# Attention and a Fourier layer on one core: the sums of the first Fourier stage are made earlier and kept in DRAM

## The chip, the cores and the metric

The kernel runs on one core of a Trainium2 chip. The time is device time in microseconds (us). The engines are TensorE (PE; PEld is its weight load), VectorE (DVE), ScalarE (ACT), GpSimd (POOL), and SyncE (SP), which issues every DMA of this kernel.

## The reference

Two independent halves share the inputs' shape of 2048 tokens by 1024, and their outputs are joined side by side:

```
qkv = x @ wqkv                         # 32 heads of 32
p = softmax(q k^T / sqrt(32)); o = p v
A = o @ wo
a, b = xB @ Wd_re^T, xB @ Wd_im^T      # Fourier matrices, hidden
B = C_re @ a - C_im @ b                # Fourier matrices, sequence
out = concat(A, B)
```

## The kernel before, in words

All products outside the attention ("fills") are in single precision. Each operand is split into a high and a low part (`halves`, L543), and each pair of operands costs three 128x128x512 matmuls: high by high, low by high, high by low. Products of 2x2 blocks are done with 7 instead of 8 block products, so that operands are often sums or differences of blocks.

The fills stand in one list that fixes their order: the projections q, k, v (`qkv`, L643, steps x = 0 to 11), the first Fourier stage (`dense1`, L1250: the input's transpose times the sequence matrices), the second (`dense2`), and the output projection. The attention's matmuls come in three streams: S (L1586, the pass that finds the maxima), T (L1711, the transposed scores) and V (L1741, probabilities by values). S, T and V are laid between the fills.

That order is made by a planner (`Plan`), which runs all engines on a clock of its own with a cost for each instruction. On POOL, DVE, ACT and SP it takes the ready operation with the lowest rank, which is the number of fill groups listed so far. Each engine then runs its list strictly in that order, SP too: a DMA that must wait holds all later DMAs. Tiles are numbered as the planner hands them out, whichever engine writes them, so the numbers of two engines tell which came first in its plan.

Steps that matter here:

- `fetch` (L488) makes a sum of blocks: a DMA for the first block (L511, into `raw`, or `er` while x < 5), one for each further block (L520, into `g`, or `raw` while x < 5), an add on POOL or DVE (L530), and, if the sum is used again, a DMA that stores it (L538). `raw` has 6 buffers, `g` 4, `er` 8; all are handed out in turn.
- `piece` (L559) fetches a stationary operand of 128x512 (four 128x128 weights) and splits it: the high half `h` on ACT (L549) or DVE (L550), the low half `l` on POOL or DVE (L553). `moving` (L585) does the same for the other operand, into `slot` tiles.
- `qkv` step x = 3: six groups on q and k, then eight on v (t = 0 to 7), each of 12 matmuls. Step x = 4 begins with three weights (two groups each), made from a block of `wqk` and a stored block `sq_d`.
- `dense1` runs its seven block products in the order 1, 2, 5, 6, 7, 4, 3. Products 1 and 3 are cut once more into seven (`split`, L1320), the others are whole (`simple`, L1269). The stationary sums of products 5, 6, 7 (and 3) were fetched at their own product: 8 pieces each in `simple`, 2 each in `split`. Sum 5 was stored in `s1_d`, 6 in `s2_d`, the base of product 3 in `s4_d` (made in product 7), the inner sums 5 and 6 in `w5_d`, `w6_d`.

Of the kernel before, what the change touches and what calls it, by code (L numbers as in the profile page):

```python
# [8 lines left out]
F32 = mybir.dt.float32  # L9
# [7 lines left out]
P = 128  # L17
# [207 lines left out]
def kernel(  # L225
# [168 lines left out]
    SPLIT = (1,3)  # L394
# [222 lines left out]
    class Acc:  # L617
# [5 lines left out]
        def at(self):  # L623
            return self.get()[:, self.half]
# [15 lines left out]
    CR = Ring(NCR)  # L640
    CR.users = [att_gate for _ in range(NCR)]

    def qkv():  # L643
        VR, SG = Ring(NV), Ring(2)
        sq, tx, t1x = ([[] for _ in range(8)] for _ in range(3))
# [267 lines left out]
        for x, (p, blocks, v) in enumerate(STEPS[:10]):  # L913
            spare[0] = x < 5
            if x == 0:
                where[0] = ahead
                W = []
                for c in range(4):
                    W.append(blocks_piece(c))
                    load_x(0, c)  # L920
                qk_groups(W, 0)
                for k in range(4, 8):
                    load_x(0, k)
                qk_groups(W, 1)
                for c in range(4):
                    load_v_weight(0, c)
            for i, b in enumerate(blocks if x else ()):
                where[0] = ahead if x < 5 else within
                W = piece(w_terms(p, lambda i, j: wqk[b + 8 * i][:, 4 * j : 4 * j + 4, :], sq_d[b], sq[b]), (sq_d[b], sq[b]) if p == 6 else None)
                if x > 5 and i == 0:  # L930
                    for k in range(4, 8):
                        load_x(x, k)
                qk_group(x, W, b, 0)
                qk_group(x, W, b, 1)
                if x < 5:
                    for k in range(8 * i // len(blocks), 8 * (i + 1) // len(blocks)):
# [12 lines left out]
            if x == 4:  # L949
                for u in ahead[0].users + slots[32:]:  # L950
                    att_gate.extend(u)
                for i in range(12, 16):
                    slots[i] = list(att_gate)
            if x == 9:
                for c in range(4):
                    load_v_weight(10, c)
        for x in (10, 11):
            for t in range(8):
                v_group(x, t)
                if x == 11 and t < 4:  # L960
                    load_x(11, 4 + t)
                elif x == 10 and t < 2:
                    for k in range(2):
                        load_x(10, 4 + 2 * t + k)
                elif x == 10 and 2 <= t < 6:
                    load_x(11, t - 2)
                    load_v_weight(11, t - 2)
        for b in range(8):
            W = [piece(w_terms(p, lambda i, j: wqk[b + 8 * i][:, 4 * j : 4 * j + 4, :], None, None)) for p in (7, 4)]
            for n in range(2):  # L970
                qk_group(10, W[0], b, n)
                qk_group(11, W[1], b, n)

    ORDER = (1, 2, 6, 7, 5, 3, 4)

# [272 lines left out]
    steps = [0]  # L1248

    def dense1():  # L1250
        s4 = [[[] for _ in range(2)] for _ in range(4)]
        t2 = [[[] for _ in range(8)] for _ in range(4)]
        s2 = [[[] for _ in range(2)] for _ in range(4)]
        s2_d = [[dram.tile([P, 4, P], F32, name=f"s2_d{m}_{k}") for k in range(2)] for m in range(4)]
        s4_d = [[dram.tile([P, 4, P], F32, name=f"s4_d{m}_{k}") for k in range(2)] for m in range(4)]
# [3 lines left out]
        s1, t1 = [[[] for _ in range(2)] for _ in range(4)], [[[] for _ in range(8)] for _ in range(4)]  # L1259
        s1_d = [[dram.tile([P, 4, P], F32, name=f"s1_d{m}_{k}") for k in range(2)] for m in range(4)]  # L1260
        t1_d = [[dram.tile([P, NB], F32, name=f"t1_d{n}_{c}") for c in range(8)] for n in range(4)]
        xq = lambda d, s: (xb[d, :, s : s + 4, :], [])
        cq = lambda e, s, n: (ct[e, s, :, n * NB : n * NB + NB], [])
        step = steps

# [2 lines left out]

        def simple(p):  # L1269
            def a(m, k):  # L1270
                q = lambda r, kk: xq(4 * r + m, 8 * kk + 4 * k)
                return split_a(p, q, (s1_d[m][k], s1[m][k]), (s2_d[m][k], s2[m][k]))

            def b(n, c):
                q = lambda k, e: cq(e, 8 * k + c, n)
                return split_b(p, q, (t1_d[n][c], t1[n][c]), (t2_d[n][c], t2[n][c]))

            keep_a = {5: lambda m, k: (s1_d[m][k], s1[m][k]), 6: lambda m, k: (s2_d[m][k], s2[m][k])}.get(p, lambda m, k: None)
            keep_b = {5: lambda n, c: (t1_d[n][c], t1[n][c]), 6: lambda n, c: (t2_d[n][c], t2[n][c])}.get(p, lambda n, c: None)
            A = {}  # L1280
            for n in range(4):
                z = step[0]
                step[0] += 1
                M = []

                def load(m, k):
                    if n == 0:
                        A[m, k] = held(fetch([P, 4, P], a(m, k), keep_a(m, k)), None if m < 2 else 12 + 2 * m + k)

                for k in range(2):  # L1290
                    load(0, k)
                    for c in range(4 * k, 4 * k + 4):
                        M.append(moving((8 * z + c) % 12, b(n, c), keep_b(n, c)))
                for m in range(1, 4):
                    for k in range(2):
                        load(m, k)
                for m in range(4):
                    h = DONE_IN.get(p)
                    out_to = to(h, m, n) if h else (None, None)
                    group(((chunk(A[m, k], c), (M[4 * k + c], whole)) for k in range(2) for c in range(4)), 8,  # L1300
                          outer(p, X[m][n], Y[m][n], *out_to, h is not None and h[1] == 1))
                    if p == 7 and 3 in SPLIT and m % 2:
                        i, k = divmod(2 * n + m // 2, 2)
                        fetch([P, 4, P], [(1, *xq(i, 8 + 4 * k)), (-1, s2_d[i][k], s2[i][k])], (s4_d[i][k], s4[i][k]))

        def stays():
            box = {}
# [10 lines left out]
            return k  # L1318

        def split(i):  # L1320
            def base_a(m, k):
                return (s4_d[m][k], s4[m][k]) if i == 3 else xq(m, 8 * (i - 1) + 4 * k)

            def base_b(c, n):
                return cq(*{1: (0, c), 2: (0, 8 + c), 3: (1, 8 + c)}[i], n)

            w, w_d = {}, {}
            for p in (5, 6):
                for n in range(2):
                    w[p, n], w_d[p, n] = [], dram.tile([P, 4, P], F32, name=f"w{p}_d{i}_{n}")  # L1330
# [5 lines left out]
            for j in WITHIN:  # L1336
# [481 lines left out]
    while nf < len(fills) or any(place[n] < len(s) for n, s in streams.items()):  # L1818
# [27 lines left out]
        held = False  # L1846
# [96 lines left out]
```

## Time and profile before

| | |
|---|---|
| median of 3 runs | 2926.0 us (2925.46 to 2927.98) |
| the profiled execution | 2924.82 us, its span 2923.0 us |
| PE, share of the span | 100% (weight loads 73%) |
| ACT, DVE, POOL | 79%, 77%, 38% |
| DMA, 16 engines | 67.8%; 636.24 MB |
| TensorE clock | 1.0 of full speed throughout |

Busy time of PE is read with care: a matmul of 512 columns is shown 389 ns long, though the next one starts 227 ns after it. So a gap in the rows of PE is shorter than the time that was really lost there.

### The profile page before, as it was taken

To read this page: it belongs to the slowest core of one execution; us is meant where nothing else is said; L and a number is where in the kernel's file an instruction comes from. 1 tells how busy PE (TensorE), PEld (TensorE's weight loads), DVE (VectorE), ACT (ScalarE), POOL (GpSimd) and SP (SyncE) were. 2 spreads that over 40 slices of the span, in tenths; PEclk is the share of its full clock that TensorE was granted. 3 is DMA by queue.
4 is the path that set the end of the run, shared out by engine and by line. 5 is a ranking of instruction groups with operands and counts; after the bars stand their busy time and mean duration, and the time that the engine had idled before them with its cause. 6 is when DMAs were issued, how large, how long until landed. Compare 5 with 4: busy or idle time off the path is not lost.

```text
span 2923.0 us, 46116 instructions
## 1 busy us (share of the span) xinstructions
PE 2911.5 (100%) x14826; PEld 2130.8 (73%) x14826; DVE 2260.2 (77%) x3072; ACT 2297.2 (79%) x4369; POOL 1107.2 (38%) x866
## 2 busy tenths in 40 slices
PE   9999999999999999999999999999999999999999
PEld 7887777776667776777776777777677777777787
DVE  7778888788889768777778787778877877876496
ACT  5348888888899888888888888988888888887532
POOL 2323335222365124243434342347613653342042
PEclk9999999999999999999999999999999999999999
DMA  9975658766687448678869775568735776663463
GB/s 340 372 241 186 201 183 280 231 214 223 220 263 227 146 136 274 219 241 273 277 224 286 227 240 170 155 192 281 231 98 172 255 238 189 188 189 123 124 241 140
DMA packets 444956, 636.24 MB, mean 218 GB/s; under 512 B 115726, under 2 KB 150286, under 8 KB 444590
## 3 DMA queue, kind: packets, MB, share of 16 engines
q1 hardware_dynamic: 444716, 633.29, 67.8%
q8 instruction: 120, 1.97, 0.3%
q14 instruction: 120, 0.98, 0.1%
HBM read 448.56 MB, written 184.57 MB: 217 GB/s over the span
## 4 chain that ended last, share of the span: by engine, by line
PE 94%; ACT 2%; DMA 2%; DVE 1%; issue 1%; SPq 0%; DVEq 0%; ACTq 0%
PE pd L433 43%; PE psT L1711 16%; PE psS L1586 15%; PE pd L1741 14%; PE psT L433 6%; ACT psS L1595 1%; ACT pt L1718 1%; DMA qs<-m_d 0%; DMA m_d<-lt 0%; DVE negm L1592 0%; DMA raw<-in_ct 0%; PE psT L455 0%; DMA er<-in_xa 0%; DMA qs<-qk_d 0%; DMA er<-in_wv 0%
## 5 line engine op out<-in xcount | busy, mean ns | idle before, releaser
L1592 DVE TENSOR_REDUCE negm<-psS 128x1 f32<-128x1024 f32 x1024 | 1242.4, 1220 | 255.9 <-PE psS L1586 244.6
L1595 ACT ACTIVATE psS<-psS,negm 128x1024 f32<-128x1024 f32 x1024 | 1230.0, 1201 | 75.2 <-DVE negm L1592 69.5
L1718 ACT ACTIVATE pt<-psT 128x512 f32<-128x512 f32 x1656 | 1000.8, 705 | 267.4 <-PE psT L1711 243.8
L433 PE MATMUL pd<-slot,h 128*128 128x512 f32 x2704 | 921.3, 390 | 0.0
L1711 PE MATMUL psT<-qs,ks 128*128 128x512 f32 x2048 | 794.5, 394 | 2.3 <-ACT pt L1718 1.3
L553 POOL TENSOR_TENSOR slot<-raw,slot 128x512 fp32r<-128x512 f32 x278 | 357.6, 1292 | 776.1 <-DVE slot L550 424.2
L433 PEld LDWEIGHTS pd<-slot,h 128*128 128x128 f32 x2704 | 507.5, 188 | 106.1 <-issue 0.8
L530 POOL TENSOR_TENSOR raw<-raw,g 128x512 f32<-128x512 f32 x321 | 414.8, 1302 | 428.4 <-issue 78.1
L433 PE MATMUL pd<-slot,l 128*128 128x512 f32 x1352 | 526.7, 390 | 0.0
L1711 PEld LDWEIGHTS psT<-qs,ks 128*128 128x128 f32 x2048 | 381.9, 188 | 142.0 <-issue 42.7
L1586 PE MATMUL psS<-ks,qs 128*128 128x512 f32 x1552 | 474.0, 391 | 2.5 <-ACT psS L1595 2.2
L433 PE MATMUL pd<-slot,slot 128*128 128x512 f32 x1560 | 436.3, 389 | 0.0
L1741 PE MATMUL pd<-pt,vt 128*32 128x512 f32 x3312 | 408.2, 594 | 0.0
L1586 PEld LDWEIGHTS psS<-ks,qs 128*128 128x128 f32 x1552 | 290.0, 188 | 67.0 <-ACT psS L1595 6.2
L433 PEld LDWEIGHTS pd<-slot,slot 128*128 128x128 f32 x1560 | 292.8, 188 | 60.8
L1595 ACT ACTIVATION_READ_ACCUMULATOR psS<-psS,negm 128x1 f32 x1024 | 328.2, 321 | 0.0
L433 PEld LDWEIGHTS pd<-slot,l 128*128 128x128 f32 x1352 | 253.8, 188 | 52.3
L1718 ACT ACTIVATE ptm<-psT 128x512 f32<-128x512 f32 x392 | 242.4, 716 | 48.9 <-PE psT L1711 47.1
L1741 PEld LDWEIGHTS pd<-pt,vt 128*32 128x32 f32 x3312 | 108.6, 110 | 231.8 <-issue 217.2
L553 POOL TENSOR_TENSOR l<-raw,h 128x512 fp32r<-128x512 f32 x105 | 135.5, 1290 | 224.5 <-PE psT L1711 79.0
L550 DVE CAST slot<-raw 128x512 fp32r<-128x512 f32 x364 | 168.0, 482 | 6.2 <-DMA raw<-in_wo 3.1
L1586 PE MATMUL psS<-ks,qx 128*128 128x512 f32 x496 | 150.1, 393 | 1.0 <-ACT psS L1595 1.0
(158 smaller groups left out, 2066.0 us busy)
## 6 DMA issues: line engine op xcount, KB each, us to landing
raw<-in_ct SPq DMA_DIRECT2D x212, 256.0 KB
g<-in_ct SPq DMA_DIRECT2D x148, 256.0 KB
raw<-ut_d SPq DMA_DIRECT2D x112, 256.0 KB
qk_d<-e SPq DMA_DIRECT2D x52, 512.0 KB
qs<-qk_d SPq DMA_DIRECT2D x128, 192.0 KB
ks<-qk_d SPq DMA_DIRECT2D x128, 192.0 KB
c<-xx_d SPq DMA_DIRECT2D x80, 256.0 KB
c<-u_d SPq DMA_DIRECT2D x72, 256.0 KB
```

The lines of the kernel that those rows point to most:

```text
L433: nc.tensor.matmul(box["ps"], a[1]((a[0].hi, a[0].lo)[u]()), b[1]((b[0].hi, b[0].lo)[v]()), start=k == 0, stop=k == n - 1)
L530: return (nc.gpsimd if e == "POOL" else nc.vector).tensor_tensor(out=dest(), in0=x, in1=y, op=ALU.add if sign > 0 and not turned else ALU. ...
L550: return nc.vector.tensor_copy(hi(), raw())
L553: return (nc.gpsimd if e == "POOL" else nc.vector).tensor_tensor(out=lo(), in0=raw(), in1=f(hi()), op=ALU.subtract)
L1586: nc.tensor.matmul(p[:, i * NB : i * NB + NB], (QX[0] if own else QS[h % 2])[:, qt * P : qt * P + P], KS[h % 2][:, c * 1024 + i * NB : c * ...
L1592: nc.vector.tensor_reduce(out=ST["negm"][:, c, qt : qt + 1], in_=box["p"], axis=AX.X, op=ALU.max, negate=True)
L1595: nc.scalar.activation(box["p"], box["p"], AF.Exp, bias=ST["negm"][:, c, qt : qt + 1], accum_out=ST["sums"][:, c, qt : qt + 1])
L1711: nc.tensor.matmul(box["p"], KS[h % 2][:, t * P : t * P + P], QS[h % 2][:, j * NB : j * NB + NB], start=True, stop=True)
L1718: nc.scalar.activation(box["t"], box["p"], AF.Exp)
L1741: nc.tensor.matmul(po["p"][j * DH : j * DH + DH, :], VT[h][:, k, :], box["t"], start=(k == t0), stop=(k == t), tile_position=(0, j * DH),)
```

## The change

`presum(key)` makes one stationary sum with `fetch` and always stores it, in a DRAM tile of its own (`sums_...` for the eight pieces of a whole product, `sum1_...` and `sum3_...` for the two of an inner one). `beside(what, n)` makes the next n sums of a list, and is called after groups of other stages: the eight inner sums of product 1 in the v groups of step x = 3; the eight sums 5 in the v groups of steps 10 and 11; the eight sums 6 in the q and k groups behind them; sums 7 and 3 (16) in product 2; the eight inner sums of product 3 in product 4. At their own product, `a` and `inner_a` then give one term, the stored sum, so that `fetch` is one DMA (L511) with no add.

The diff, cut to its core (the calls of `beside` stand inside the loops named above):

```diff
+    BESIDE = {"x":of_inner(1),"v":of_all(5),"qk":of_all(6),2:of_all(7)+of_all(3),4:of_inner(3)}
+    def presum(key):
+        what, i, m, k = key
+        if key in sums_of:
+            return
+        if i in (6, 3):
+            presum((what, {6: 5, 3: 6}[i], m, k))
...
+        terms = split_a(i, q, sums_of.get((what, 5, m, k), ()), sums_of.get((what, 6, m, k), ()))
+        to = sums_of[key] = dram.tile([P, 4, P], F32, name=f"sum{what}_{i}_{m}_{k}"), []
+        fetch([P, 4, P], terms, to)
...
+                if x == 3:
+                    beside("x", 1)
...
             def a(m, k):
-                q = lambda r, kk: xq(4 * r + m, 8 * kk + 4 * k)
-                return split_a(p, q, (s1_d[m][k], s1[m][k]), (s2_d[m][k], s2[m][k]))
+                if p in (5, 6, 7, 3):
+                    presum(("s", p, m, k))
+                    return [(1, *sums_of["s", p, m, k])]
+                return split_a(p, lambda r, kk: xq(4 * r + m, 8 * kk + 4 * k), (), ())
...
-                    if p == 7 and 3 in SPLIT and m % 2:
-                        i, k = divmod(2 * n + m // 2, 2)
-                        fetch([P, 4, P], [(1, *xq(i, 8 + 4 * k)), (-1, s2_d[i][k], s2[i][k])], (s4_d[i][k], s4[i][k]))
+                    beside(p, 1)
...
-                    A.append(piece(split_a(j, lambda r, k: base_a(2 * r + n, k), at(5, n), at(6, n)), at(j, n) if j in (5, 6) else None))
+                    A.append(piece(inner_a(j, n)))
```

The order is made anew by the planner. First place, SP late in the q and k groups and in the v groups of step x = 3, before (`u_d` stores come from finished groups; `er<-in_wqk` and `raw<-sq_d` are the weights of step x = 4):

```order
L511 DMA er_1906<-in_wv 128x512
L520 DMA raw_1912<-sq_d0_201 128x512
L829 DMA u_d1_4_234<-acc0_782 128x512
L511 DMA er_1923<-in_wqk 128x512
L511 DMA raw_1931<-in_xa 128x512
L511 DMA er_1938<-in_wqk 128x512
L829 DMA u_d2_4_237<-acc1_790 128x512
L511 DMA raw_1949<-in_xa 128x512
L520 DMA raw_1958<-sq_d1_202 128x512
L511 DMA er_1967<-in_wqk 128x512
```

The same weights after:

```order
L538 DMA sum1_7_1_0_363<-er_2033 128x512
L861 DMA u_d18_4_285<-acc4_991 128x512
L511 DMA er_2096<-in_wqk 128x512
L520 DMA raw_2103<-sum1_6_1_0_361 128x512
L861 DMA u_d19_4_288<-acc4_991 128x512
L520 DMA raw_2112<-sq_d0_201 128x512
L511 DMA er_2118<-in_wqk 128x512
L538 DMA sum1_3_0_0_364<-er_2051 128x512
L861 DMA u_d20_4_291<-acc5_1051 128x512
L511 DMA raw_2134<-in_xa 128x512
L511 DMA raw_2139<-in_xa 128x512
L520 DMA raw_2146<-sq_d1_202 128x512
```

The 24 DMAs of eight inner sums now stand among the loads from `er<-in_wv` on; the first weight's second block went from between the stores of q and k groups 0 and 1 (`u_d0`, `u_d1`) to behind that of the v group t = 3 (`u_d19`), and behind the load `er_1855<-in_wv` (`er_1839` before) it is the 42nd transfer of 256 KB. The third weight's second block, `sq_d2`, is the 56th.

Second place, ACT there, before, with the high halves of the last weight of step x = 3 (`h_1864`) and of the first two of step x = 4 (`h_1988`, `h_2016`):

```order
L549 ACTIVATE h_1864<-er_1774 128x512
L549 ACTIVATE slot36_1904<-er_1839 128x512
L549 ACTIVATE slot37_1929<-er_1872 128x512
L549 ACTIVATE slot38_1952<-er_1886 128x512
L549 ACTIVATE slot39_1964<-er_1906 128x512
L549 ACTIVATE h_1988<-er_1923 128x512
L549 ACTIVATE h_2016<-er_1938 128x512
```

And after, where `h_2160` and `h_2216` are those two:

```order
L549 ACTIVATE slot39_2054<-er_1995 128x512
L549 ACTIVATE h_2160<-er_2096 128x512
L549 ACTIVATE slot0_2167<-raw_2134 128x512
L549 ACTIVATE slot1_2174<-raw_2139 128x512
L549 ACTIVATE slot2_2205<-raw_2176 128x512
L549 ACTIVATE h_2216<-er_2118 128x512
```

`h_1864` is numbered between the PE banks `pd_1848` and `psT_1879`, the first two groups of step x = 3. The second weight's cast of step x = 4 now stands behind three casts of loads for a later step. PE at the seam of the two steps, after (the last v group of step x = 3 writes `psT_2165`, the first group of step x = 4 `psT_2192`):

```order
L433 MATMUL psT_2165<-slot19_1688,slot7_1547 128x512 x3
L433 MATMUL psT_2192<-slot8_1736,h_2160 128x512
L433 MATMUL psT_2192<-slot8_1736,l_2171 128x512
L433 MATMUL psT_2192<-slot8_1736,h_2160 128x512
L433 MATMUL psT_2192<-slot9_1743,h_2160 128x512
```

The low half `l_2171` has a higher number than the last v group's bank; before, the halves `h_1988` and `l_1996` were numbered ahead of the bank of the first v group, `psT_2006`.

Third place, SP at the start of product 1, before (`w5_d1_0` is its first inner sum, stored and loaded again for sum 6; `w5_d1_0_0` and the like are sums of the moving operand):

```order
L538 DMA w5_d1_0_574<-raw_9066 128x512
L520 DMA g_9147<-in_ct 128x512
L511 DMA raw_9153<-in_xb 128x512
L538 DMA w5_d1_0_0_575<-raw_9073 128x512
L520 DMA g_9172<-in_xb 128x512
L538 DMA w5_d1_0_1_576<-raw_9077 128x512
L520 DMA g_9192<-in_ct 128x512
L538 DMA w5_d1_0_2_577<-raw_9087 128x512
L520 DMA g_9208<-in_ct 128x512
L511 DMA raw_9220<-w5_d1_0_574 128x512
```

And after:

```order
L511 DMA raw_9174<-in_ct 128x512
L511 DMA raw_9180<-in_ct 128x512
L511 DMA raw_9186<-sum1_5_0_0_358 128x512
L511 DMA raw_9194<-in_ct 128x512
L1720 DMA vt_9201<-v_d0_126 128x4x32
L511 DMA raw_9212<-in_ct 128x512
L511 DMA raw_9230<-in_ct 128x512
```

The loads from `in_xb` and the store and reload of the stationary sum are gone there; one load of the stored sum stands in their place. On PE the number of matmuls of each kind is the same in both.

## Rows read from the trace of the kernel before

**Rows 1.** The page, busy us of each engine, share of the span, instructions.

```profile
PE 2911.5 (100%) x14826; PEld 2130.8 (73%) x14826; DVE 2260.2 (77%) x3072; ACT 2297.2 (79%) x4369; POOL 1107.2 (38%) x866
```

**Rows 2.** The page, the chain that ended last, by engine.

```profile
PE 94%; ACT 2%; DMA 2%; DVE 1%; issue 1%; SPq 0%; DVEq 0%; ACTq 0%
```

**Rows 3.** The chain in order of time: start us, us, what.

```profile
24.02 2.72 PE pd L433 x12
32.19 5.44 PE pd L433 x24
...
550.79 5.50 DMA m_d<-lt
556.35 3.19 DMA qs<-m_d
...
794.46 5.13 DMA raw<-in_ct
...
1028.95 7.00 PE pd L1741 x64
```

**Rows 4.** Waits of PE, 560 to 2520 us: us in total, times, longest.

```profile
PE psS L1586 <- ACT psS L1595: 3.2, 9, 0.6
PE psT L1711 <- ACT pt L1718: 1.3, 2, 1.1
PE psT L1711 <- DMA qs<-m_d: 0.8, 2, 0.5
```

**Rows 5.** Waits of PE, 795 to 805 us, in product 1.

```profile
PE psT L1711 <- ACT pt L1718: 1.1, 1, 1.1
```

**Rows 6.** Waits of PE, 2040 to 2120 us, end of product 3.

```profile
PE psS L1586 <- ACT psS L1595: 1.9, 5, 0.6
```

**Rows 7.** Timeline of PE, the seam of steps x = 3 and 4.

```profile
159.31 2.88 PE L433 MATMUL psT<-slot,slot 128*128 128x512 f32 x12
162.03 0.39 PE L433 MATMUL psT<-slot,h 128*128 128x512 f32 x1
162.26 0.39 PE L433 MATMUL psT<-slot,l 128*128 128x512 f32 x1
```

**Rows 8.** Timeline, low halves of the first and third weight of x = 4.

```profile
139.72 0.69 DVE L553 TENSOR_TENSOR l<-er,h 128x512 fp32r<-128x512 f32 x1
...
156.17 1.30 POOL L553 TENSOR_TENSOR l<-er,h 128x512 fp32r<-128x512 f32 x1 [3.39 <-ACT h L549]
```

**Rows 9.** Stretches: us, busy of each engine, PEclk, DMA share, GB/s.

```profile
120.00:140.00 20.00, 20.00 (x90) 16.57 (x89) 16.86 (x21) 8.19 (x14) 8.69 (x7) 1.00 1.00 361
140.00:162.00 22.00, 22.00 (x98) 18.22 (x98) 11.97 (x18) 5.51 (x9) 3.88 (x3) 1.00 0.76 271
162.00:184.00 22.00, 22.00 (x98) 18.21 (x97) 14.01 (x23) 4.62 (x8) 1.29 (x1) 1.00 0.96 331
184.00:260.00 76.00, 76.00 (x337) 62.92 (x336) 67.84 (x90) 52.21 (x94) 25.02 (x20) 1.00 0.53 156
...
480.00:560.00 80.00, 79.66 (x415) 56.97 (x414) 65.34 (x88) 68.35 (x132) 42.02 (x33) 1.00 0.86 283
970.00:1100.00 130.00, 130.00 (x671) 95.31 (x670) 88.99 (x109) 113.56 (x221) 25.47 (x20) 1.00 0.42 125
```

**Rows 10.** Timeline of SP, the load ahead of the first added one.

```profile
123.86 0.38 SPq L511 DMA_DIRECT2D er<-in_wv  x1
```

**Rows 11.** Timeline, a group of x = 3 on PE and a cast on ACT.

```profile
123.95 0.39 PE L433 MATMUL pd<-slot,h 128*128 128x512 f32 x1
...
128.22 0.61 ACT L549 ACTIVATE h<-er 128x512 fp32r<-128x512 f32 x1
```

**Rows 12.** Groups of POOL and PE: xcount, busy us, mean ns, idle before.

```profile
L530 POOL TENSOR_TENSOR raw<-raw,g 128x512 f32<-128x512 f32 x321 | 414.8, 1302 | 428.4 <-issue 78.1 <-DMA raw<-in_ct 60.7 <-DMA g<-in_ct 33.9
...
L1741 PE MATMUL pd<-pt,vt 128*32 128x512 f32 x3312 | 408.2, 594 | 0.0
...
L1741 PE MATMUL pd<-ptm,vt 128*32 128x512 f32 x784 | 125.5, 593 | 0.0
```

More of the change, by code (lines that the diff above doesn't have):

```diff
@@ L641, with of_all, of_inner, beside @@
     CR.users = [att_gate for _ in range(NCR)]
+    xq = lambda d, s: (xb[d, :, s : s + 4, :], [])
+    sums_of = {}
+    def presum(key):
[4 more added lines that the diff above has]
+            presum((what, {6: 5, 3: 6}[i], m, k))
+        if what == "s":
+            q = lambda r, kk: xq(4 * r + m, 8 * kk + 4 * k)
+        else:
+            q = lambda r, kk: sums_of["s", 3, 2 * r + m, kk] if what == 3 else xq(2 * r + m, 8 * (what - 1) + 4 * kk)
+        terms = split_a(i, q, sums_of.get((what, 5, m, k), ()), sums_of.get((what, 6, m, k), ()))
+        to = sums_of[key] = dram.tile([P, 4, P], F32, name=f"sum{what}_{i}_{m}_{k}"), []
+        fetch([P, 4, P], terms, to)
+    def of_all(p):
+        return [("s", p, m, k) for m in range(4) for k in range(2)]
+    def of_inner(i, ps=(5, 6, 7, 3)):
+        return [(i, p, n, 0) for p in ps for n in range(2)]
+    BESIDE = {"x":of_inner(1),"v":of_all(5),"qk":of_all(6),2:of_all(7)+of_all(3),4:of_inner(3)}
+    def beside(what, n):
+        todo = BESIDE.get(what, [])
+        for key in todo[:n]:
+            presum(key)
+        del todo[:n]
     def qkv():
@@ L959, in qkv @@
                 v_group(x, t)
+                if t % 2:
+                    beside("v", 1)
                 if x == 11 and t < 4:
@@ L972, in qkv @@
                 qk_group(11, W[1], b, n)
+                beside("qk", 1)
     ORDER = (1, 2, 6, 7, 5, 3, 4)
@@ L1250, in dense1 @@
     def dense1():
-        s4 = [[[] for _ in range(2)] for _ in range(4)]
         t2 = [[[] for _ in range(8)] for _ in range(4)]
-        s2 = [[[] for _ in range(2)] for _ in range(4)]
-        s2_d = [[dram.tile([P, 4, P], F32, name=f"s2_d{m}_{k}") for k in range(2)] for m in range(4)]
-        s4_d = [[dram.tile([P, 4, P], F32, name=f"s4_d{m}_{k}") for k in range(2)] for m in range(4)]
         t2_d = [[dram.tile([P, NB], F32, name=f"t2_d{n}_{c}") for c in range(8)] for n in range(4)]
@@ L1258, in dense1 @@
         X, Y = ([[Far(v[m][n]) for n in range(4)] for m in range(4)] for v in (xx_d, yy_d))
-        s1, t1 = [[[] for _ in range(2)] for _ in range(4)], [[[] for _ in range(8)] for _ in range(4)]
-        s1_d = [[dram.tile([P, 4, P], F32, name=f"s1_d{m}_{k}") for k in range(2)] for m in range(4)]
+        t1 = [[[] for _ in range(8)] for _ in range(4)]
         t1_d = [[dram.tile([P, NB], F32, name=f"t1_d{n}_{c}") for c in range(8)] for n in range(4)]
-        xq = lambda d, s: (xb[d, :, s : s + 4, :], [])
         cq = lambda e, s, n: (ct[e, s, :, n * NB : n * NB + NB], [])
@@ L1276, in b @@
                 return split_b(p, q, (t1_d[n][c], t1[n][c]), (t2_d[n][c], t2[n][c]))
-            keep_a = {5: lambda m, k: (s1_d[m][k], s1[m][k]), 6: lambda m, k: (s2_d[m][k], s2[m][k])}.get(p, lambda m, k: None)
             keep_b = {5: lambda n, c: (t1_d[n][c], t1[n][c]), 6: lambda n, c: (t2_d[n][c], t2[n][c])}.get(p, lambda n, c: None)
@@ L1287, in load @@
                     if n == 0:
-                        A[m, k] = held(fetch([P, 4, P], a(m, k), keep_a(m, k)), None if m < 2 else 12 + 2 * m + k)
+                        A[m, k] = held(fetch([P, 4, P], a(m, k)), None if m < 2 else 12 + 2 * m + k)
                 for k in range(2):
@@ L1320, in split, with inner_a @@
         def split(i):
-            def base_a(m, k):
-                return (s4_d[m][k], s4[m][k]) if i == 3 else xq(m, 8 * (i - 1) + 4 * k)
             def base_b(c, n):
                 return cq(*{1: (0, c), 2: (0, 8 + c), 3: (1, 8 + c)}[i], n)
+            def inner_a(j, n):
+                if j in (5, 6, 7, 3):
+                    presum((i, j, n, 0))
+                    return [(1, *sums_of[i, j, n, 0])]
+                base = lambda r, k: sums_of["s", 3, 2 * r + n, k] if i == 3 else xq(2 * r + n, 8 * (i - 1) + 4 * k)
+                return split_a(j, base, (), ())
             w, w_d = {}, {}
@@ L1329, in split @@
                 for n in range(2):
-                    w[p, n], w_d[p, n] = [], dram.tile([P, 4, P], F32, name=f"w{p}_d{i}_{n}")
                     for c in range(4):
```

## The prediction

> **What bounds the kernel now.** I read the busy line first, then the chain, then the waits of the engine that the chain names. The busy line shows PE at 2911.5 of 2923.0 us [rows 1]; since its matmul rows overlap, that alone proves little. The chain settles it: 94% of the way back from the last instruction is PE, and DMA is 2% [rows 2]. In order of time the chain's long pieces are fills at an even pace, 24 in 5.44 us or 0.2267 us each, and the attention's V matmuls, 64 in 7.00 us [rows 3]. The granted clock is 1.00 in all stretches that I cut [rows 9]. The change leaves the number of matmuls as it is. So it can only win what PE loses waiting, and it can only cost what new waiting it brings.
>
> What PE loses waiting from 560 to 2520 us, a stretch that holds all of the first Fourier stage, is small: 3.2 + 1.3 + 0.8 = 5.3 us in 13 waits [rows 4]. A wait in these rows is short by the overlap, a matmul of 0.39 us [rows 7] less the pace of 0.2267 us, so 0.16 us; 13 of them are 2.1 us. The ceiling of a gain is therefore about 7.4 us.
>
> **The change part by part.** First what it removes. At product 1 the wait of 1.1 us [rows 5] is the end of a row of causes: a load of a Fourier block took 5.13 us on the chain [rows 3], its cast on ACT waited, an exponential stood behind that cast, and PE behind the exponential. There, as the order shows, two loads and a store of each inner sum become one load. At the end of product 3, five waits on ACT make 1.9 us [rows 6]. With the overlap, 6 x 0.16 = 1.0 us, the two cut products hold 1.1 + 1.9 + 1.0 = 4.0 us. I take two thirds as saved, 2.7 us, since these waits lie where the sums were made, but are named as ACT's, and ACT's exponentials stay. Of the other 7.4 - 4.0 = 3.4 us I take a third, 1.1 us: the whole products lose a burst of 8 second loads (and of 8 stores in products 5 and 6) each, and the adds of the pieces, but two of the waits left are on the small transfer of the maxima (`qs<-m_d`), which any other DMA can delay. Gain: 3.8 us, between nothing and 7.4.
>
> The adds only move: 48 before, 48 after (32 for the whole products, 16 for the cut ones). On POOL, where most run, one takes 1.302 us [rows 12], and POOL is 38% busy [rows 1]. Were the same adds on DVE, they would cost 48 x 0.69 (the length of a like DVE subtraction [rows 8]) = 33 us of an engine with 23% of its span, 663 us, free. Nothing for either. DMAs grow by 40 loads and 16 stores of 256 KB, 14.7 MB, since a stored sum is read once more and four more kinds are stored (whole sum 7, inner sums 7 and 3 of both cut products). Over the whole span that hides; what counts is where they stand.
>
> Step x = 3 is the place where they may cost something. Eight inner sums bring 24 transfers, 6.29 MB. At the full rate of the stretch before, 361 GB/s at a DMA share of 1.00 [rows 9], they take 17.4 us. From 140 to 162 us only 0.24 x 22 = 5.3 us are free, from 162 to 184 us only 0.9, from 184 to 260 us then 0.47 x 76 = 36 us [rows 9]. So some 12 us of transfers slide past the seam at 162 us, and the weights of x = 4 are in that line. Before, the first one's low half was ready at 139.72 + 0.69 = 140.4 us [rows 8], 21.9 us ahead of its use at 162.26 us [rows 7]; the third at 157.5 us [rows 8], against a need four groups of 2.72 us later, 173.1 us. After, the order puts the first low half behind the opening of the last v group (159.31 us [rows 7]), so it is at most 2.95 us ahead.
>
> Does it arrive? The second block of the first weight is the 42nd transfer behind the one that SP issued at 123.86 us [rows 10]: 11.0 MB at 361 GB/s are 30.5 us, so 154.4 us, plus the 5.13 us that a load under traffic took [rows 3] is 159.5 us; add, cast and subtraction (0.69, 0.61 and 1.30 us [rows 8, 11]) make it 162.1 us, need 162.26. The third weight, the 56th transfer: 40.7 us, so 164.6, with the same sums 172.3 us, need 173.1. It fits, with 0.2 and 0.8 us to spare. Against that stands how late this chip runs behind the planner when DMAs are dense. The last weight's cast of x = 3 was planned between the first group (123.95 us) and the second, 2.72 us later, and ran at 128.22 us [rows 11], 1.5 to 4.3 us late, which that time cost nothing. With such lateness the low half, which the plan starts between 159.31 and 162.26 - 1.30 = 160.96 us, would end between 162.1 and 166.6 us: a wait of 0 to 4.3 us, once, since the later weights are late by the same. I take 1.0 us, near the end that the count of transfers gives. A gain is excluded here: PE has no wait in this stretch.
>
> Each inner sum 6 needs the stored sum 5 first, and each sum 3 the stored sum 6. A small store and the load that reads it back took 5.50 and 3.19 us on the chain (`m_d<-lt`, `qs<-m_d`) [rows 3]; two such pairs in a row are 17 us, inside the 22 us of the eight v groups, and nobody but their buffers waits for them.
>
> In the v groups of steps 10 and 11 (480 to 560 us) DMA is already 0.86 busy at 283 GB/s [rows 9], so 329 at full share. Another 24 transfers take 19 us, and 0.14 x 80 = 11 us are free. The 8 us that are left move into the time behind. The fills' operands come far ahead there; what can be late is one head's pair of small transfers, on which PE waits already. Bounds: 0 and 8 us, if one head took it all; I take 0.8 us, twice the mean of the two waits of that kind, 0.8 / 2 [rows 4]. In product 2 (970 to 1100 us) 48 transfers take 35 us at 361 GB/s, and 0.58 x 130 = 75 us are free [rows 9]: nothing. The q and k groups and product 4 take 24 each; nothing, or the same 0.4 us for one wait, inside the rounding.
>
> The sum against the profiled execution: 2924.8 - 3.8 + 1.0 + 0.8 = 2922.8 us. That execution was 1.2 us below the median of the runs, so on their scale 2924.0 us.
>
> **The rivals.** Second: the waits only change place. PE's 13 waits are small, spread, and end on ACT or on DMAs that the change doesn't touch. A plan made anew may lose as much at other seams: 2926 to 2928 us. For it speaks that no wait names a stationary sum; against it, that 3.0 of 5.3 us stand in the two cut products.
>
> Third, slower: the line of DMAs before the seam at 162 us runs below full rate, and PE stands at x = 4. Before, at share 0.96, the stretch behind the seam moved 331 GB/s [rows 9]. At 331 the third weight would be ready at 123.86 + 44.4 + 5.13 + 2.6 = 176 us, a wait of 2.9 us; at 300 GB/s the 48.9 us make it 180.5 us, 7.4 us late. It decides from about 310 GB/s down: with no gain elsewhere, 2932 to 2934 us. Its second weight is open to the same, its cast being queued behind three others. For it speaks the thin margin; against it, that the stretch just before, full of the same 256 KB blocks, moved 361 GB/s.
>
> Fourth: more hidden waiting goes than the waits show. By full paces, the 14826 matmuls [rows 1] are 3312 + 784 = 4096 of V [rows 12], 448 us at 7.00 us per 64, and 10730 others; less the 82 ahead of the steady start at 24.02 us [rows 3], 10648 x 0.2267 = 2413.9 us. With the 24.0 us this is 2886 us, 37 less than the span. Most of that I hold to be the change between V and the other shapes, which stays. If a quarter of it fell with the sums, the time is near 2917 us. The Trainium skill, Perfetto Trace Analysis, Identifying the Most-Contended Engine, says that matmul busy time misleads and that the weight loads' share tells the headroom; that is 73% here, so it would speak for this case. Against it: the pieces of the chain run at an unbroken 0.2267 us, so the missing 27% are no idle time that a sooner operand fills.
>
> **How the numbers follow.** What this kernel's measurement can tell from no change is about 0.2%, 5.9 us: below 2920.1 us is faster, above 2931.9 slower. The forecast (2920.5 to 2926) has 0.55, waits that change place (2926 to 2930) 0.25, the late weights (2931 and more) 0.12, hidden waiting (about 2917) 0.08. Faster: the last and the forecast's lower edge, 0.12. Slower: most of the third, 0.12. Same: 0.76. The range: low, all 7.4 us of waits gone, 2918.5 us; high, nothing gained, 4.3 us at the seam and some 1.5 us in the v groups, 2932 us.
>
> **What would show it.** Right: in the profile after, PE's waits from 795 to 805 us and from 2040 to 2120 us are mostly gone; at the seam near 162 us PE waits at most about a microsecond; the chain stays PE by 94% or more; transfers total near 651 MB; the DMA share from 140 to 184 us is near 1. Wrong: a wait of several microseconds on the halves `h` or `l` between 160 and 175 us (third case); as many microseconds of waits on ACT as before, in other places (second); a PE pace other than 0.2267 us, or a granted clock below 1.00, which nothing here leads me to expect.

## The result and the profile after

The changed kernel takes 2935.17 us in the median (2933.34 to 2938.02, 7 runs) against 2926.96 us (2925.12 to 2927.98, 7 runs) of the kernel before on the same chip: a ratio of 1.0030, 95% interval 1.0018 to 1.0042 (ratios here are estimated from all runs, so they differ a little from those of the medians). It is slower by some 8 us, where I had forecast 2924.0 and no measurable difference. Its profiled execution took 2933.34 us with a span of 2931.5, the fastest of its seven.

The page of the profile after, its busy line and its chain by engine, answer to [rows 1, 2]:

```profile
PE 2912.7 (99%) x14826; PEld 2133.0 (73%) x14826; DVE 2244.6 (77%) x3059; ACT 2296.5 (78%) x4361; POOL 1135.9 (39%) x887
PE 90%; DMA 6%; DVE 2%; SPq 1%; ACT 1%; issue 0%; POOL 0%; DVEq 0%; ACTq 0%; POOLq 0%
```

PE does as many matmuls as before, and the chain now runs through DMAs for 6% of the span instead of 2%. So more of that way back leads through transfers. PE's waits after, from 560 to 2520 us (total, times, longest), against [rows 4]:

```profile
PE psT L1744 <- ACT pt L1751: 5.2, 2, 3.7
PE psS L1619 <- ACT psS L1628: 2.2, 2, 1.2
PE psT L1744 <- DMA qs<-m_d: 2.1, 2, 1.4
```

There are 6 waits where there were 13, but 9.5 us of them instead of 5.3. The wait of 3.7 us alone is half the ceiling of the gain. The five waits at 2040 to 2120 us [rows 6] are gone, as forecast, but the one at product 1 [rows 5] has stayed and grown. From 795 to 810 us:

```profile
PE psT L1744 <- ACT pt L1751: 1.5, 1, 1.5
```

The stretches that took the new transfers, after, against [rows 9]: us, busy of each engine, granted clock, DMA share, GB/s.

```profile
140.00:162.00 22.00, 22.00 (x98) 18.21 (x97) 10.42 (x16) 1.08 (x2) 2.59 (x2) 1.00 0.98 357
162.00:184.00 22.00, 20.31 (x87) 15.91 (x86) 15.66 (x22) 9.84 (x17) 9.03 (x7) 1.00 1.00 363
184.00:260.00 76.00, 76.00 (x336) 62.64 (x336) 66.96 (x92) 47.47 (x82) 27.09 (x21) 1.00 0.66 209
480.00:560.00 80.00, 79.22 (x425) 54.33 (x421) 65.23 (x87) 68.11 (x130) 47.26 (x37) 1.00 0.96 331
```

From 140 to 184 us the DMAs are full, and PE is busy for 20.31 of the 22 us behind the seam, where it was busy for all of them.

To find all of the loss I worked out from the two traces PE's time over its pace: from the start of each matmul to the start of the next, less the usual time of that pair of kinds in these traces (0.227 us; 0.318 us into a V matmul, 0.522 us out of one; pairs of V matmuls left out), summed where it is over 0.06 us. The sum over the span is 22.9 us before and 31.3 us after: the 8.4 us between them are the difference of the spans, 8.5 us. By stretch, the changed kernel adds 2.6 us at 100 to 260 us (the seam), 2.6 at 480 to 660 (the V groups and just behind), 1.2 at 1110 to 1160 (late in product 2, where the operands of product 5 are fetched), 5.5 at 1980 to 2035 (early in product 3), and saves 3.4 at 2035 to 2125 (its end). The other stretches together change by -0.1 us.

The largest of these is one wait. The timelines of ACT, SP and PE around it, after (start us, us, what, idle before and its releaser):

```profile
1989.38 0.38 SPq L511 DMA_DIRECT2D raw<-sum  x1
...
1989.95 1.09 ACT L1751 ACTIVATE pt<-psT 128x512 f32<-128x512 f32 x2 [3.71 <-PE psT L1744]
1995.20 0.63 ACT L549 ACTIVATE h<-raw 128x512 fp32r<-128x512 f32 x1 [4.16 <-DMA raw<-sum]
1995.74 1.07 ACT L1751 ACTIVATE pt<-psT 128x512 f32<-128x512 f32 x2
...
1996.37 0.50 PE L1744 MATMUL psT<-qs,ks 128*128 128x512 f32 x1 [3.72 <-ACT pt L1751]
```

A stored inner sum of product 3 is loaded at 1989.38 us. ACT has its cast next in its order and stands for 4.16 us until the load has landed; the two exponentials behind the cast come late, and PE waits 3.72 us for their bank. The chain of after shows what came before it, three transfers in a row:

```profile
1976.76 5.91 DMA c<-yy_d
1982.68 5.51 DMA qs<-qk_d
...
1989.38 5.80 DMA raw<-sum
```

In the code the planner gives a 256 KB load 256 / 360 + 1.6 = 2.3 us, if nothing is queued ahead of it; here it took 5.80 us. Before, such a sum was added on POOL or DVE after its loads, and `MARGIN` puts those engines 2 us behind a landing. A stored sum needs no addition, so ACT's cast follows the bare load, and ACT's margin is 0.

### The profile page after: what moved, and what is told of

The parts are those of the page before. It is cut to its first block, busy times and chain, and to the rows that moved or that the text cites. A ratio compares the mean times of both kernels' runs of the same rounds, so it can differ in the third digit from the quotient of the medians.

```text
span 2931.5 us, 46182 instructions
## 1 busy us (share of the span) xinstructions
PE 2912.7 (99%) x14826; PEld 2133.0 (73%) x14826; DVE 2244.6 (77%) x3059; ACT 2296.5 (78%) x4361; POOL 1135.9 (39%) x887
## 2 busy tenths in 40 slices
DMA packets 453021, 650.94 MB, mean 222 GB/s; under 512 B 116622, under 2 KB 151182, under 8 KB 452654
## 4 chain that ended last, share of the span: by engine, by line
PE 90%; DMA 6%; DVE 2%; SPq 1%; ACT 1%; issue 0%; POOL 0%; DVEq 0%; ACTq 0%; POOLq 0%
PE pd L433 41%; PE psT L1744 16%; PE psS L1619 15%; PE pd L1774 14%; PE psT L433 4%; DMA qs<-qk_d 1%; DMA raw<-in_xa 1%; DMA er<-in_xa 1%; DMA raw<-sums 1%; DVE negm L1625 0%; DMA er<-in_xb 0%; DMA c<-u_d 0%; DVE er L530 0%; ACT psS L1628 0%; ACT slot L549 0%
## 5 line engine op out<-in xcount | busy, mean ns | idle before, releaser
L530 POOL TENSOR_TENSOR raw<-raw,g 128x512 f32<-128x512 f32 x328 | 424.8, 1303 | 443.0 <-DMA raw<-in_ct 78.3
L553 POOL TENSOR_TENSOR l<-raw,h 128x512 fp32r<-128x512 f32 x113 | 145.9, 1291 | 295.5 <-PE pd L433 93.3
```

Of the source, the lines that this page charges most:

```text
L530: return (nc.gpsimd if e == "POOL" else nc.vector).tensor_tensor(out=dest(), in0=x, in1=y, op=ALU.add if sign > 0 and not turned else ALU. ...
L553: return (nc.gpsimd if e == "POOL" else nc.vector).tensor_tensor(out=lo(), in0=raw(), in1=f(hi()), op=ALU.subtract)
```

## The experiments

Theory 1 was that chain, together with the waits at the seam. Rival A was the seam alone. Rival B, later theory 2, was that any new order has more waits, whatever is changed. Theory 3 (the change alone costs) and theories 4 and 5 (each list has a price or a gain at its own place) came later. In the table, list 4 is the list of product 4, the x list that of step x = 3, the v list that of the V groups; the late lists are those of products 2, 7 and 4; inner 1 are the sums of the x list, made in another place. Each comparison shares its chip with runs of the kernel before. The last five columns are PE's time over its pace in us, from one profiled execution each (in e4, e6, e8 and e18 the slowest of the runs): at 100-260, 480-660, 1980-2035, 2035-2125 us, and in all.

| kernel | median us | ratio (95%) | 100 | 480 | 1980 | 2035 | all |
|---|---|---|---|---|---|---|---|
| before | 2926.96 | 1 | 0.0 | 1.3 | 0.2 | 4.1 | 22.9 |
| after | 2935.17 | 1.0030 (1.0018-1.0042) | 2.6 | 3.9 | 5.7 | 0.7 | 31.3 |
| e1 after, ACT margin | 2940.83 | 1.0056 (1.0043-1.0070) | 5.8 | 9.7 | 0.9 | 0.3 | 36.1 |
| e2 before, ACT margin | 2932.76 | 1.0023 (1.0015-1.0032) | 0.0 | 1.8 | 4.5 | 5.5 | 28.8 |
| e3 without x list | 2933.27 | 1.0025 (1.0014-1.0036) | 0.0 | 3.3 | 4.2 | 2.6 | 29.7 |
| e4 without list 4 | 2936.39 | 1.0043 (1.0030-1.0055) | 5.4 | 4.7 | 2.3 | 6.2 | 38.3 |
| e5 before, redrawn | 2935.40 | 1.0030 (1.0018-1.0041) | 0.0 | 2.1 | 1.3 | 7.0 | 29.4 |
| e6 before, redrawn | 2930.80 | 1.0020 (1.0012-1.0029) | 0.0 | 0.8 | 1.7 | 5.5 | 31.3 |
| e12 before, redrawn | 2925.22 | 0.9998 (0.9990-1.0007) | 0.0 | 1.2 | 1.1 | 4.2 | 21.7 |
| e7 after, redrawn | 2950.00 | 1.0083 (1.0069-1.0097) | 2.2 | 2.0 | 5.3 | 1.9 | 44.8 |
| e8 after, redrawn | 2940.79 | 1.0049 (1.0036-1.0062) | 3.3 | 8.5 | 1.7 | 2.6 | 36.0 |
| e13 after, redrawn | 2931.72 | 1.0018 (1.0009-1.0027) | 2.7 | 7.0 | 1.8 | 0.8 | 30.3 |
| e9 list 4 alone | 2924.19 | 0.9994 (0.9986-1.0003) | 0.0 | 0.7 | 1.2 | 1.4 | 21.7 |
| e14 the same, redrawn | 2927.66 | 1.0006 (0.9997-1.0014) | 0.0 | 1.1 | 2.2 | 0.7 | 22.3 |
| e10 late lists | 2926.75 | 1.0001 (0.9992-1.0010) | 0.0 | 1.6 | 1.9 | 2.1 | 26.5 |
| e16 late and v lists | 2929.34 | 1.0012 (1.0003-1.0020) | 0.0 | 3.5 | 2.4 | 1.7 | 24.7 |
| e11 late and x lists | 2931.98 | 1.0020 (1.0011-1.0029) | 1.9 | 0.8 | 2.1 | 3.4 | 28.1 |
| e15 inner 1 in q, k groups | 2923.39 | 0.9993 (0.9984-1.0001) | 0.0 | 1.6 | 0.9 | 1.7 | 20.9 |
| e17 the same, redrawn | 2921.30 | 0.9990 (0.9982-0.9999) | 0.0 | 1.6 | 0.3 | 1.1 | 18.9 |
| e18 two lists | 2925.16 | 1.0001 (0.9992-1.0010) | 0.0 | 2.0 | 2.6 | 0.2 | 26.0 |

### e1 and e2: time for the landing on ACT

```diff
-    MARGIN = {"POOL": 2, "DVE": 2, "ACT": 0}
+    MARGIN = {"POOL": 2, "DVE": 2, "ACT": 2}
```

> The changed kernel with one number of the planner changed: a step of ScalarE that waits for a landing is planned 2 us after it instead of at once, as steps of POOL and DVE already are. Theory 1 (a stored sum comes by a bare load whose high half is cast on ScalarE with nothing planned between, and the exponentials queue behind that cast when the load is late): the wait of 3.7 us and its 1.4 us of slow matmuls at 1996 us go, 2935.2 - 5.1 = 2930 us (2928 to 2932). Rival A (the crowded DMAs at the seam, 140 to 184 us, where three inner sums of the first split product are made, are the loss): nothing there changes, 2934 to 2936. Rival B (any redrawing of the plan moves the waits by some us, whatever is redrawn): anywhere from 2927 to 2938, and the kernel before with the same number moves as much.

> The kernel before with the same number of the planner changed (ScalarE 2 us after a landing). Theory 1: in it the casts of summed pieces stand behind an addition that already has its 2 us, so few steps gain, 2925.5 to 2928. Rival A: the same. Rival B: it moves by more than 3 us from 2927, to either side.

The wait at 1996 us went: 1980 to 2035 us fell from 5.7 to 0.9 us. But the time did not fall to 2930; it rose to 2940.83, above every range that I had written, that of rival B too. PE's waits of e1 from 480 to 660 us show two of what took its place:

```profile
PE pd L1774 <- DVE e L787: 3.0, 1, 3.0
PE pd L1774 <- DVE e L735: 3.0, 1, 3.0
```

And the same number made the kernel before slower by 0.23%, at other places: 1980 to 2035 us holds 4.5 us there, none of it behind a stored sum of the change. So theory 1 names the wait rightly, but not the whole of the 8 us: a planner number that only moves instructions costs nearly as much as the change did. Rival B was hit on e2.

### e3 and e4: one list taken back

```diff
-BESIDE = {"x":of_inner(1),"v":of_all(5),"qk":of_all(6),2:of_all(7)+of_all(3),4:of_inner(3)}
+BESIDE = {"v":of_all(5),"qk":of_all(6),2:of_all(7)+of_all(3),4:of_inner(3)}        # e3
+BESIDE = {"x":of_inner(1),"v":of_all(5),"qk":of_all(6),2:of_all(7)+of_all(3)}      # e4
```

> The changed kernel without the list of step x = 3: the inner sums of the first split product are formed in that product as in the kernel before, all other lists stay. Theory 1: the three waits at the seam (0.90 + 0.99 + 0.30 = 2.2 us) go and the one at 1996 stays, 2933 us (2931.5 to 2934.5). Rival A: at least 5 us come back, 2930 or less. Rival B: 2927 to 2938.

> The changed kernel without the list of product 4: the inner sums of the last split product are formed in that product as in the kernel before, all other lists stay. Theory 1: the 5.3 us at 1996 go, and the 3.1 us of short waits at 2040 to 2120 come back, 2935.2 - 5.3 + 3.1 = 2933 us (2930 to 2934). Rival A: only the 3.1 us come back, 2936 to 2939. Rival B: 2927 to 2938.

e3 met theory 1's number, 2933.27, and its seam is clean, but the waits it lost came back elsewhere, and its interval overlaps that of after: the time alone decides nothing, but rival A, which had 2930 or less here, is out. In e4 the 1996 wait went and the waits at the end of product 3 came back (6.2 us), both as expected; its 2936.39 lies outside theory 1's range and inside rival A's, 2936 to 2939. Its order is that of after on every engine until past 1700 us, and still its seam cost 5.4 us in the profiled execution, where after's cost 2.6.

### e5 to e8: the same work in another order

```diff
-    MM, PV, SWITCH, TINY = 0.2274, 0.8535, 0.363, 0.17
+    MM, PV, SWITCH, TINY = 0.2276, 0.8535, 0.363, 0.17      # e5, e7; 0.2272 in e6, e8
```

> The kernel before, with the planner's length of one matmul at 0.2276 us instead of 0.2274: the same work and the same bytes, only the drawn order differs in many places. Theory 2 (the plan of the kernel before is a draw with few waits, and any redrawing finds more): 2929 to 2936, 3 us or more above 2926. Theory 3 (the change has a price of its own, at the seam, by the V groups at 480 to 600 us and where bare loads meet ScalarE, and a redrawing costs nothing): within 2 us of 2926.

> The same with 0.2272 us. Theory 2: 2929 to 2936. Theory 3: within 2 us of 2926.

> The changed kernel with the length of one matmul at 0.2276 us in the plan. Theory 2: 2928 to 2940, as far from 2935 as the redrawings of before are from 2926, and on the mean no slower than those. Theory 3: 2933 to 2938, the seam and the V groups at 480 to 600 us keep their waits of 2 us or more each, and the mean lies 6 us or more above the redrawings of before.

> The same with 0.2272 us. Theory 2: 2928 to 2940. Theory 3: 2933 to 2938, with waits of 2 us or more at the seam and again at 480 to 600 us.

Both theories hold half. The kernel before with another order is 0.2 to 0.3% slower, against theory 3. But the changed kernel's orders lie higher again, against theory 2's mean, and e7 and e8 lie above the ranges of both. With e12 and e13 below, four orders of each: ratios 1, 1.0030, 1.0020, 0.9998 with a mean of 1.0012, and 1.0030, 1.0083, 1.0049, 1.0018 with a mean of 1.0045. The means differ by 0.33%, about 10 us, yet single orders of one kernel differ by about 10 us (before) and 19 us (after), so four of each don't settle that number. The last two are also redrawn only in part: by the traces e12 keeps the order of before up to 643 us, and e13 that of after up to 418 us.

### e9 to e12: the lists added one by one

```diff
+BESIDE = {7:of_all(3),4:of_inner(3)}                               # e9
+BESIDE = {2:of_all(7),7:of_all(3),4:of_inner(3)}                   # e10
+BESIDE = {"x":of_inner(1),2:of_all(7),7:of_all(3),4:of_inner(3)}   # e11
-    MAX, EVAC, CAST, BIT = 1.22, 0.685, 0.415, 0.275
+    MAX, EVAC, CAST, BIT = 1.22, 0.686, 0.415, 0.275               # e12
```

Sums that no list names are formed as in the kernel before; `7:of_all(3)` stands where that kernel makes the same sums.

> Of the change only the list of product 4 is left: the inner sums of the last split product are made beside product 4 and stored, all other sums are formed as in the kernel before. Theory 4 (each list has a price or gain at its own place, beside what a redrawing costs): nothing above the kernel before at the seam or at 480 to 660 us, and 2035 to 2125 us loses 3.9 us of waits, so 2922 us without a redrawing's cost, and at most 2930 with it. Theory 2 (redrawing alone rules): 2929 to 2936, like the redrawings of the kernel before.

> The lists of the dense products without the V and score groups: the sums of products 7 and of the last split product are made beside products 2, 7 and 4, products 5 and 6 and the first split product form theirs as in the kernel before. Theory 4: as the one before, 2922 to 2930, nothing at the seam or at 480 to 660 us. Theory 2: 2929 to 2936.

> The same with the list of step x = 3 put back (the inner sums of the first split product are made at 140 to 184 us and stored). Theory 4: waits of 2.2 to 5.8 us at 100 to 260 us, none above the kernel before at 480 to 660 us, 2 to 6 us above the run without this list. Theory 2: 2929 to 2940, the difference to the run without the list of either sign.

> The kernel before with the planner's length of an evacuation at 0.686 us instead of 0.685: same work, other order, fewer rows moved than by a change of the matmul's length. Theory 2: 2928 to 2934. Theory 3 (a redrawing costs nothing by itself): 2925 to 2928.

The list of product 4 alone costs nothing that this measurement can tell, and gives about 0.1% at most: theory 4. The list of step x = 3, put back, costs 1.0020 against 1.0001 on the same chip, intervals that don't touch, but only 1.9 us of it stand at the seam in the profile, a little under theory 4's 2.2; the rest is spread, and both are single orders. e12 went against theory 2: a smaller redrawing cost nothing.

### e13 to e16: order, place, and the V groups

```diff
-    MAX, EVAC, CAST, BIT = 1.22, 0.685, 0.415, 0.275
+    MAX, EVAC, CAST, BIT = 1.221, 0.685, 0.415, 0.275                 # e13, on the changed kernel
+    MAX, EVAC, CAST, BIT = 1.22, 0.687, 0.415, 0.275                  # e14, on e9
+BESIDE = {"qk":of_inner(1),2:of_all(7),7:of_all(3),4:of_inner(3)}     # e15
+BESIDE = {"v":of_all(5),2:of_all(7),7:of_all(3),4:of_inner(3)}        # e16
```

> The changed kernel with the planner's length of a maximum at 1.221 us instead of 1.220: same work, other order. Theory 5 (the lists of step x = 3 and of the V groups stand where the DMAs are nearly full, and each has its price in any order): 2933 to 2941, with 2 us or more of waits at 100 to 260 us and again at 480 to 660 us. Theory 2 (the order drawn alone rules): as likely under 2932 as over it.

> The version with the list of product 4 alone, with the planner's length of an evacuation at 0.687 us instead of 0.685. Theory 5: 2922 to 2930, no waits at 100 to 260 us, at most 2.5 us at 480 to 660 us and at most 2.6 us at 2035 to 2125 us. Theory 2: 2929 to 2936.

> The late lists, with the inner sums of the first split product made beside the score groups at 600 to 795 us (one before each group) instead of in step x = 3. Theory 5 (the place is the price): no waits at 100 to 260 us, 2926 to 2930. Rival (the price is the stored sums' bare loads at the first split product): 2930 to 2934, with 3 us or more of waits at 790 to 1110 us.

> The late lists and the list of the V groups (the sums of product 5 made at 480 to 600 us); the sums of product 6 and of the first split product as in the kernel before. Theory 5: 3 to 8 us of waits at 480 to 660 us against 1.6 without this list, 2929 to 2934. Theory 2: no more there than without, 2925 to 2936.

e15 is the clearest run of all. The same sums of the first split product, stored and loaded again just as in e11, but made in another place, give 0.9993 (0.9984-1.0001) against 1.0020 (1.0011-1.0029). The time is below theory 5's range of 2926 to 2930 and below the rival's, and reading the stored sums at product 1 cost nothing: 790 to 1110 us holds 2.8 us by the pace in e15, 2.7 before. So it is the place of that list that has the price, as far as one order of e11 and two of this version (e17 is the second) can show it. The stores ran from 543 to 624 us, sooner than I had written, for the most part through a stretch that had room. Its window in the kernel before, and then in e17, the redrawn e15:

```profile
560.00:600.00 40.00, 40.00 (x198) 30.33 (x197) 27.73 (x30) 36.85 (x73) 1.29 (x1) 1.00 0.46 142
```

```profile
560.00:600.00 40.00, 40.00 (x198) 30.36 (x197) 27.97 (x29) 36.74 (x72) 7.75 (x6) 1.00 0.71 231
```

The DMA share rises from 0.46 to 0.71, and PE stays busy throughout. At 89 GB/s more, these 40 us took some 3.6 of the list's 6.3 MB. In e16 the list of the V groups stands where the share is 0.86 already [rows 9]; it brings 3.5 us of waits to 480 to 660 us against 1.6 in e10. The time, 1.0012 against 1.0001, agrees, with intervals that overlap. What it holds up there is not a small transfer but an evacuation. DVE and PE in e16:

```profile
525.45 0.69 DVE L787 TENSOR_TENSOR e<-c,pd 128x512 f32<-128x512 f32 x1 [2.55 <-DMA c<-u_d]
...
526.20 1.06 PE L1780 MATMUL pd<-pt,vt 128*32 128x512 f32 x8 [2.06 <-DVE e L787]
```

The chain of e16 has the load behind it, a stored partial sum that the V group adds:

```profile
519.37 5.99 DMA c<-u_d
```

e13 again has both crowded places (2.7 and 7.0 us), though with 2931.72 it came below theory 5's range. e14 kept within it.

### e17 and e18: a better version, once more in another order

```diff
+    MAX, EVAC, CAST, BIT = 1.222, 0.685, 0.415, 0.275                 # e17, on e15
+BESIDE = {"qk":of_inner(1),7:of_all(3),4:of_inner(3)}                 # e18
+    MAX, EVAC, CAST, BIT = 1.22, 0.684, 0.415, 0.275                  # e18
```

> The late lists and the inner sums of the first split product beside the score groups, in another order (a maximum planned at 1.222 us instead of 1.220). Theory 5 (the place was the price): no waits at 100 to 260 us, 2922 to 2929, under the 2932 of the list in step x = 3. Theory 2 (a lucky order): 2929 to 2936.

> Only two lists: the inner sums of the first split product beside the score groups and those of the last beside product 4; all dense sums as in the kernel before (an evacuation planned at 0.684 us instead of 0.685). Theory 5: 2921 to 2928, waits of at most 2.6 us at 2035 to 2125 us and none at 100 to 260 us. Theory 2: 2929 to 2936.

e17, a little below theory 5's 2922 to 2929, takes 2921.30 us against 2923.69 of the kernel before on that chip, 0.9990 (0.9982-0.9999): the only version here whose interval lies below 1, and faster than both kernels, though by less than the 0.2% that I hold for certain. e18 equals the kernel before; its waits are low where the lists act, and 1160 to 1980 and 2125 us to the end hold 5.9 and 5.6 us of its 26.0.

What the runs show together: in 7 kernels with the list of step x = 3 the seam has 1.9 to 5.8 us of waits, in the 13 without it none. In 8 kernels with the list of the V groups 480 to 660 us has 2.0 to 9.7 us, in the 12 without 0.7 to 2.1. In 14 kernels with the list of product 4 the end of product 3 has 0.2 to 3.4 us, in the 6 without 4.1 to 7.0. So these prices and this gain stay through the redrawings, with ranges that hardly meet. Not all of these are different orders: after, e4, e11 and e13 have the same one at the seam, so the 7 kernels there are four orders, and ten of the 13 without the list share that of before.

At 1980 to 2035 us the sums don't part, 0.3 to 5.7 us with the list of product 4 and 0.2 to 4.5 without, but the causes do. In 8 of the 14 kernels with that list (after, e3, e7, e8, e11, e14, e16, e18) ACT's cast stands 1.5 to 7.9 us for the load of a stored inner sum, and PE waits 1.0 to 3.7 us for the exponential behind it. In the six without the list ACT waits for no load at all in this stretch, and PE's waits have other causes. ACT and PE in e18:

```profile
1984.52 0.63 ACT L549 ACTIVATE h<-raw 128x512 fp32r<-128x512 f32 x1 [5.81 <-DMA raw<-sum]
1985.69 0.50 PE L1749 MATMUL psT<-qs,ks 128*128 128x512 f32 x1 [1.51 <-ACT pt L1756]
```

So the 8 us of the changed kernel are two crowded places, of 2.6 us each in its profile, less the gain of 3.4 us, and waits behind the loads of stored sums, 5.5 and 1.2 us, whose length this order happens to have. How much of the whole a luckier order would win back stays open: the best of four orders, e13, is still some 5 us above the kernel before.

## Why the prediction was wrong, point by point

**What bounds the kernel** was right: PE's matmuls stayed, and the whole difference is PE's waiting, with a slower clock behind the longest wait. The transfers came to 650.94 MB, as forecast.

**The gain, 3.8 us.** At the end of product 3 it came in full, 3.4 us by the pace. The ceiling of 7.4 us was too low, since PE also loses time that its rows don't show as waits: by the pace 560 to 2520 us held 16.0 us before. After, it holds 20.2. At product 1 nothing came: PE waited 1.5 us there instead of 1.1. The chain of after has a load of a Fourier block at that place, as before [rows 3]:

```profile
797.62 5.35 DMA raw<-in_ct
```

I had put that wait down to the loads of the sums because it stood where the sums are made; the chain already named the Fourier block, which the change doesn't touch.

**The step that failed** is the one that counted "two loads and a store become one load" as a gain alone. I priced how the sums are made and where, and never how they are read: a load under traffic, and on its landing an engine that works in order. This was to be seen in the rows that I used for product 1, a cast on ACT behind a load of 5.13 us with an exponential behind it [rows 3, 5]; at product 3 the change made more of just that. In place of a gain the runs showed a wait: 5.5 us at product 3 in this order, the clock's fall included, and waits of the same making in 8 of 14 kernels, against none at product 1 in e15. That such a load is waited for is shown; how long depends on the order, and whether the reading costs anything on the mean of many orders is not. A second place is late in product 2, 1.2 us, where the chain of after holds a stored sum's load and DVE's cast of it; only the order of after and e4 has it:

```profile
1133.02 4.77 DMA raw<-sums
```

**The seam, 1.0 us, bounds 0 and 4.3.** After has 2.6 us there, by two waits and small change. PE's waits from 100 to 260 us:

```profile
PE pd L433 <- POOL l L553: 0.8, 1, 0.8
PE psT L433 <- POOL l L553: 0.7, 1, 0.7
```

The mechanism was right, the term too small, and "once, since the later weights are late by the same" was wrong: two weights were waited for, each by itself, and a third for 0.3 us. e1 and e4 passed the upper bound with 5.8 and 5.4 us. My count of transfers left 0.2 and 0.8 us to spare at the full rate of 361 GB/s; the stretch then ran at 357, so the rate nearly held. But the count had the first weight's second block under way at 154.4 us. SP issued it at 155.77, and the add, the cast and the subtraction behind it took what I had given them. From the timeline of after, the issue, the add and the low half:

```profile
155.77 0.36 SPq L520 DMA_DIRECT2D raw<-sq_d  x1
...
160.82 0.69 DVE L530 TENSOR_TENSOR er<-er,raw 128x512 f32<-128x512 f32 x1 [0.17 <-DMA raw<-sq_d]
...
162.26 1.27 POOL L553 TENSOR_TENSOR l<-er,h 128x512 fp32r<-128x512 f32 x1 [13.55 <-ACT h L549]
```

So the low half ended at 163.53 us, where I had 162.1. The second weight's cast began on ACT at 168.10 us, behind a cast that had stood 2.63 us for a load of a later step.

**The V groups, 0.8 us, bounds 0 and 8.** 2.6 us more in after: the mechanism is right in part, the term too small. The pair of small transfers that I had named went from a wait of 0.3 us to one of 1.4; the evacuation's own load, which e16 shows at length, I had not counted. PE's waits from 480 to 660 us, before and then after:

```profile
PE psT L1711 <- DMA qs<-m_d: 0.3, 1, 0.3
```

```profile
PE psT L1744 <- DMA qs<-m_d: 1.4, 1, 1.4
PE pd L1774 <- DVE e L787: 0.5, 1, 0.5
```

**The making in product 2** was rightly free: its share rose from 0.42 to 0.64, without a wait there.

**The rivals.** Nearest was the second, that the waits only change place, at 0.25; it had a price of at most some 4 us. The redrawings of the kernel before alone reach 0.3%. My sum has no term for the order drawn anew, and it has a spread as large as the effect. What I had named as its sign came: as many microseconds of waits on ACT in other places, 7.4 us from 560 to 2520 us where there had been 4.5. A granted clock below 1.00, which nothing had led me to expect, came too, behind the longest of them. The third rival had the right sign and place, but by its own rate of 310 GB/s or less it did not happen. Of the Trainium skill's rule (Perfetto Trace Analysis, Identifying the Most-Contended Engine) no run shows that headroom put to use: the weight loads' share is 73% in the fastest version, e17, as well.

## What to carry to other kernels

Price a stored value where it is read, not only where it is made: name the engine that stands next in line on its landing and what is queued behind it, with the duration of a load under traffic (4.8 to 6.0 us in the chains shown here). Move transfers by the DMA share of the stretch that receives them: the same eight sums brought waits in every order where the share had been 0.76 to 1.00, and nothing that could be measured in two orders where it had mostly been 0.46. And where a planner draws the order, time several orders of both versions before you believe a difference of 0.3%.

## What the hardware showed that I had not expected

PE's longest wait cost more than its length. After the 3.72 us without a matmul, the granted clock fell to the lower of its levels, 1.2 GHz. The stretch behind that wait, and for comparison that behind the wait of 1.5 us at 804.8 us, both after:

```profile
1997.00:2000.00 3.00, 3.00 (x8) 2.35 (x8) 0.00 (x0) 3.00 (x6) 3.00 (x4) 0.50 0.69 215
805.00:808.00 3.00, 3.00 (x14) 2.32 (x14) 2.53 (x3) 3.00 (x7) 3.00 (x3) 1.00 0.63 190
```

In 3 us PE began 8 matmuls instead of 14, which adds some 1.4 us to the 3.7. In e16 the stretch behind its wait of 2.06 us was granted 0.54:

```profile
527.00:530.00 3.00, 3.00 (x20) 0.77 (x16) 0.28 (x1) 1.21 (x2) 2.50 (x2) 0.54 0.95 332
```

And the same order can wait for different times where DMAs are full: 2.6, 5.4, 1.9 and 2.7 us at the seam in the profiled executions of after, e4, e11 and e13, whose orders are the same up to there.
